# Attention keys as three chunks of 128 and a shared rest of 64, with batch 0 in a written-out order of steps, in an attention and SwiGLU FFN kernel

## The chip, the cores and the metric

The kernel runs on one core of a Trainium2 chip. The metric is the device time of one execution in microseconds (us). Times come from repeated runs; the profile comes from one further execution that the hardware profiler recorded, and it has a time of its own.

## The reference

Softmax attention over 8 batches of 12 heads with 448 tokens and a head dimension of 64, followed by a gated FFN on the 3584 tokens with 768 features. All inputs and the output are float32.

```python
scores = q @ k.T / sqrt(64)                 # per head: 448 x 448
attn = exp(scores - max) / sum              # over keys
x = (attn @ v), heads side by side          # 3584 x 768
out = (silu(x @ w_gate) * (x @ w_val)) @ w_out   # 768 -> 1536 -> 768
```

## The kernel before

The work is cut into 48 pairs of heads, six pairs per batch. Engines: PE is TensorE (PEld its weight loads), DVE is VectorE, ACT is ScalarE, POOL is GpSimd, SP only issues transfers. All matmuls are in fp16 with fp32 sums in PSUM. Every engine runs its instructions in the order in which the program lists them; the order is written by hand and by a small planner at build time.

**One pair.** `load_qk16` and `load_v` load q, k and v with a cast from fp32 to fp16; these transfers are issued by POOL. A partition holds four neighbouring tokens of a head, so 112 partitions hold the 448 tokens, and the keys are taken as four chunks of 112. `prep` brings q and k into the layout `qkT` with the head dimension on partitions: for pairs 0 to 10 with transposes on PE (`turn`, line 199) and one copy on DVE, for pairs 11 and later (`NPE`) with two copies on POOL (line 167) and two transfers with transpose on SP (lines 170 and 174). `qk(pr, c)` makes one score unit: two matmuls with 64 rows each, one per head, in the two halves of TensorE (line 217), and one exp on ACT over both heads (line 225). `pv_chunk` multiplies the exps by v with a column of ones (line 243 and 251): eight matmuls of 65 columns per chunk into one PSUM bank `acc`. The queries of a head are 448 = 3 x 128 + 64; the rests of the two heads share one accumulator slot, with zeros in `E` between the heads. After the last chunk DVE divides by the sums (lines 262 to 274). `turn_x` turns the result into `X`, the input of the FFN: on PE for pairs below `XPE` = 12, on SP from there on. For the first two batches `turn_rests` (line 306) turns the last 64 queries of all six pairs.

**FFN.** The tokens are split into eight blocks of alternately 384 and 512. `ffn1_steps` has twelve steps per block: a group `gp` and a group `vp` of six matmuls each (line 326), a tanh on ACT (line 341) and two operations on DVE (345 and 348). `ffn2_steps` has six or eight steps per block: twelve matmuls into `op` (line 371), an eviction on ACT (378), and after two steps the stores from SP (390).

**PSUM.** [...] Three score buffers of two banks (`ps_s`) and two single banks (`ps_f`, tag `f`) that `acc`, `vp`, `op` and the turns use in rotation; `gp` sits in a score buffer, or in an `f` bank when `gate_small` is set.

**Order.** The first six pairs (`FIRST`) run in a loop over 24 score units, with the turns, V copies (`copy_v`) and PV chunks at places from the tables `XAT` and `CAT`. From then on the program goes through visits: each takes two or three score units, up to two pairs of PV that are ready (`todo`), and then FFN steps. Which FFN steps stand in a visit comes from `run_budget` for the first blocks and from `share` later. Block 0's second half (`ffn2_steps`) follows its first half at once; the second halves of later blocks wait in `ffn2_wait` until the next block is added. A block is added two visits after the PV of its batch's last pair.

**Loads.** The table `wq` says at which pair weights and early pairs are asked for: gate and value weights (`g`, `v`, four parts each) at pairs 0 to 4, the output weights `wo` (`o`) at pairs 6 and 7. Pairs from 14 on are loaded six pairs ahead (`LA`), when the score units of a pair begin. POOL's queue holds all of these loads in order, together with the copies of line 167. In the built program each load from POOL, from the ninth on, waits for the load eight before it.

Of the kernel before, what the change touches and what calls it, by code (L numbers as in the profile page):

```python
# [26 lines left out]
NX = 6  # L27
NV = 5
VS = 9
EB = 15  # L30
# [3 lines left out]
def kernel(  # L34
# [24 lines left out]
    MQ = S - D  # L59
# [13 lines left out]
    load_table("exp_and_others")  # L73

# [7 lines left out]
    ps_f = ctx.enter_context(tc.tile_pool(name="ps_f", bufs=2, space=PSUM))  # L82

    Es = [consts.tile([P, NC * EB + 1, D], FP16, name=f"E{i}") for i in range(NE)]
    Xts = [consts.tile([128, 7, D], FP16, name=f"xt{i}") for i in range(NX)]
    Xrs = [consts.tile([D, 128], FP16, name=f"xr{i}") for i in range(3)]
    Vts = [consts.tile([P, 2, NC, D + 2], FP16, name=f"vo{i}") for i in range(NV)]
    vraw = consts.tile([P, VS, 2, NC, D], FP16, name="vraw")
# [17 lines left out]
    def dummy(n):  # L106
        wp = ps_f.tile([128, 512], FP32, tag="f", name="wp")
        for _ in range(n):
            nc.tensor.matmul(wp[:], lhsT=warm[:, 0:128], rhs=warm[:], start=True, stop=True)  # L109

    def load_qk32(pr):
        rq = raws.tile([P, 2, NC, D], FP32, tag="rq", bufs=RB)
        rk = raws.tile([P, 2, NC, D], FP32, tag="rk", bufs=RB)
        for dst, src in ((rq, q), (rk, k)):
            nc.sync.dma_start(dst[:], src[0, 2 * pr : 2 * pr + 2].rearrange("h (p c) d -> p h (c d)", c=NC))
        raw[pr] = (rq[:], rk[:])
# [3 lines left out]
    def load_qk16(pr, n=2):  # L120
        h0 = 2 * (pr % 2) if pr >= 14 else 0
        if h0 == 0:
            q16 = raws.tile([P, 4, NC, D], FP16, tag="rq", bufs=RB, name="q16")
            k16 = raws.tile([P, 4, NC, D], FP16, tag="rk", bufs=RB, name="k16")
            pairbuf[:] = [q16, k16]
        q16, k16 = pairbuf
        for dst, src in ((q16, q), (k16, k)):
            flat = src.rearrange("b h s d -> (b h) s d")[2 * pr : 2 * pr + 2 * n]
            nc.gpsimd.dma_start(dst[:, ds(h0, 2 * n)], flat.rearrange("h (p c) d -> p h (c d)", c=NC))  # L129
        for i in range(n):  # L130
            h = h0 + 2 * i
            raw[pr + i] = (q16[:, h : h + 2], k16[:, h : h + 2])

    def load_v(pr, n=1):
        b, h = divmod(2 * pr, H)
        nc.gpsimd.dma_start(  # L136
            vraw[:, ds(pr % VS, n)].rearrange("p r h c d -> p (r h) (c d)"),
            v[b, h : h + 2 * n].rearrange("h (p c) d -> p h (c d)", c=NC),
        )
# [17 lines left out]
    def prep(pr):  # L157
        rq, rk = raw[pr]
        if pr == 0 or pr >= NPE:
            qk16 = attp.tile([P, 2, NC, 2, D], FP16, tag="qk16", bufs=3)  # L160
            for t, src in enumerate((rq, rk)):
                dst = qk16[:, 1 - t].rearrange("p c h d -> p h c d")
                if pr == 0:
                    nc.vector.tensor_copy(dst[:, 0], src[:, 0])
                    nc.scalar.activation(dst[:, 1], src[:, 1], AF.Copy)
                else:
                    nc.gpsimd.tensor_copy(dst, src)  # L167
        qkT[pr] = attp.tile([128, 2 * S + D], FP16, tag="qkT", name="qkT", bufs=5)
        if pr >= NPE:
            nc.sync.dma_start_transpose(  # L170
                qkT[pr][:, 0 : 2 * S].rearrange("p (c q) -> p c q", q=P),
                qk16[:].rearrange("p t c h d -> p (t c h d)"),
            )
            nc.sync.dma_start_transpose(
                qkT[pr][:, 2 * S :].rearrange("p (c q) -> p c q", c=1),
                qk16[0:D, 1, 0].rearrange("p h d -> p (h d)"),
            )
            return None

        def turn0():  # L180
            for t in range(2):
                tp = ps_s.tile([128, 2, 512], FP32, tag="s", name="tp")
                for c in range(NC):
                    for hx in range(2):
                        nc.tensor.matmul(
                            tp[ts(hx, 64), c // 2, ds(c % 2 * P, P)],
                            lhsT=qk16[:, 1 - t, c, hx],
                            rhs=ident[0:P, 0:P],
                            start=True,
                            stop=True,  # L190
                        )
                dst = qkT[pr][:, ts(1 - t, S)].rearrange("p (a x) -> p a x", a=2)
                nc.vector.tensor_copy(dst[:, 0], tp[:, 0, 0 : 2 * P])
                nc.scalar.activation(dst[:, 1], tp[:, 1, 0 : 2 * P], AF.Copy)
                if t == 0:
                    tq = tp
            nc.vector.tensor_copy(qkT[pr][:, 2 * S :], tq[:, 0, 0:D])

        def turn():
            if pr < FIRST + 2:  # L200
                tp = ps_s.tile([128, 2, 1024], FP16, tag="s", name="tp")[:, 0]
            else:
                tp = ps_f.tile([128, 1024], FP16, tag="f", name="tp")
            for i in range(2 * NC + 1):
                t, c = (1 - i // NC, i % NC) if i < 2 * NC else (0, 0)
                for hx in range(2):
                    src = raw[pr][t][:, hx, c, :]
                    nc.tensor.transpose(tp[ts(hx, 64), ts(i, P)], src, ident[0:P, 0:P])  # L208
            nc.vector.tensor_copy(qkT[pr][:], tp[:, 0 : 2 * S + D])  # L209
# [3 lines left out]
    def qk(pr, c):  # L213
        t = qkT[pr]
        s = ps_s.tile([128, 2, 512], FP32, tag="s")
        for hx in range(2):
            nc.tensor.matmul(  # L217
                s[:, hx, 0:S],
                lhsT=t[ts(hx, 64), c * P : c * P + 128],
                rhs=t[ts(hx, 64), ds(S + (1 - hx) * D, S)],  # L220
                start=True,
                stop=True,
            )
        e = Es[pr % NE][:, ds(c * EB, 16)].rearrange("p (h b) x -> p h (b x)", h=2)
        nc.scalar.activation(e[:, :, 0:S], s[0:P, :, 0:S], AF.Exp, scale=sm_scale)  # L225

    def qk_half(pr, half, between=None):
        for c in (2 * half, 2 * half + 1):
            qk(pr, c)
            if between and c % 2 == 0:  # L230
                between()
# [3 lines left out]
    def pv_chunk(pr, c):  # L235
        if c == 0:
            accs[pr] = ps_f.tile([128, 512], FP32, tag="f", name="acc")
        e = Es[pr % NE]
        vo = Vts[pr % NV]
        a7 = accs[pr][:, 0 : 7 * (D + 1)].rearrange("p (s d) -> p s d", s=7)  # L240
        for j in range(3):
            for hx in range(2):
                nc.tensor.matmul(  # L243
                    a7[:, 2 * j + hx],
                    lhsT=e[:, ds(c * EB + 9 * hx + 2 * j, 2)].rearrange("p b x -> p (b x)"),
                    rhs=vo[:, hx, c, 0 : D + 1],
                    start=c + j + hx == 0,
                    stop=False,
                )
        for hx in range(2):  # L250
            nc.tensor.matmul(  # L251
                a7[:, 6],
                lhsT=e[:, ds(c * EB + 6 + hx, 2)].rearrange("p b x -> p (b x)"),
                rhs=vo[:, hx, c, 0 : D + 1],
                start=False,
                stop=c == NC - 1 and hx == 1,
            )
        if c < NC - 1:
            return
        r = attp.tile([128, 8], FP32, tag="R", bufs=2, name="R")  # L260
        xt = Xts[pr % NX]
        nc.vector.reciprocal(r[:, 0:7], a7[:, :, D])  # L262
        n = 7 if pr < XPE else 6
        nc.vector.tensor_tensor(  # L264
            xt[:, 0:n],
            a7[:, 0:n, 0:D],
            r[:, 0:n].unsqueeze(2).to_broadcast([128, n, D]),
            ALU.mult,
        )
        if pr < XPE:  # L270
            return
        for hx in range(2):
            nc.vector.tensor_scalar(
                Xrs[pr % 3][:, ts(hx, D)], a7[ts(hx, D), 6, 0:D], r[ts(hx, D), 6:7], None, ALU.mult
            )

    def pv(pr):
        for c in range(NC):
            pv_chunk(pr, c)

    def turn_x(pr):
# [5 lines left out]
        xt = Xts[pr % NX]  # L287
        if pr < XPE:
            tp = accs[pr] if pr < FIRST else ps_f.tile([128, 512], FP32, tag="f", name="xtp")
            for j in range(3):  # L290
                nc.tensor.matmul(  # L291
                    tp[:, ts(j, 128)],
                    lhsT=xt[:, 2 * j : 2 * j + 2].rearrange("p h d -> p (h d)"),
                    rhs=ident[:],
# [3 lines left out]
            nc.vector.tensor_copy(dst[:, 0:MQ], tp[:, 0:MQ])  # L298
            return
        nc.sync.dma_start_transpose(  # L300
            dst[:, 0:MQ].rearrange("p (j q) -> p j q", j=3),
            xt[:, 0:6].rearrange("p j d -> p (j d)"),
        )
        nc.sync.dma_start_transpose(dst[:, MQ:S].rearrange("p (j q) -> p j q", j=1), Xrs[pr % 3][:])

    def turn_rests(b):
        tp = ps_f.tile([128, NHP, D], FP32, tag="f", name="rtp")
# [334 lines left out]
```

The softmax here doesn't subtract the row's maximum and nothing guards it: scores larger than these inputs give would overflow.

## Time and profile before

| what | value |
|---|---|
| median of 3 runs | 453.32 us (453.19 to 453.83) |
| profiled execution | 453.5 us, span 451.7 us, granted PE clock 0.998 |
| PE busy | 441.9 us (98%) |
| ACT busy | 238.8 us (53%) |
| DVE busy | 201.6 us (45%) |
| POOL busy | 141.8 us (31%) |
| transfers | 48.71 MB in packets, mean 108 GB/s |

The span is the time from the first to the last instruction in the profile; about 1.8 us of the profiled time lie outside it. "Busy" counts the time in which an engine works. Matmul ends are modelled, so lengths of matmuls overlap; the distance from one start to the next is the firmer number. In lists of instructions, the bracket at a line's end is the idle time before it and what ended that. For transfers the time from issue to landing is given.

How busy the transfers are in the first part of the span shows in this row of the page, the moved GB/s in 40 slices of 11.3 us (first eight): 142, 173, 200, 201, 196, 172, 174, 180.

### The profile page before, as it was taken

What the parts mean: (1) busy time and instruction counts of PE and PEld (TensorE: products, weight loads), DVE (VectorE), ACT (ScalarE), POOL (GpSimd) and SP (SyncE); (2) the same over time, 40 slices, a digit from 0 to 9 for tenths busy, and PEclk for the clock granted to TensorE, in tenths of its full rate; (3) what the DMA queues carried; (4) which work ended last, traced back from release to release, by engine and by line L of the source; (5) the groups of instructions that cost most, each with busy time, mean ns of one, the idle gap of its engine ahead of it and who ended that gap; (6) DMA issues with size and microseconds to landing.
All of it is one profiled execution on the core that took longest, in us unless ns stands there. A gap on an engine that the chain in (4) does not pass through costs nothing.

```text
span 451.7 us, 9871 instructions
## 1 busy us (share of the span) xinstructions
PE 441.9 (98%) x4024; PEld 247.0 (55%) x4024; DVE 201.6 (45%) x447; ACT 238.8 (53%) x350; POOL 141.8 (31%) x228
## 2 busy tenths in 40 slices
PE   8999999999999999999999999999999999999995
PEld 3655565545455556454555656545455666544563
DVE  3666562456654434455443534353453544055300
ACT  6965666566746465554554546644555462222221
POOL 8755715927642225252313405330100000000000
PEclk9999999999999999999999999999999999999999
DMA  9999999999969379874749758772503112200033
GB/s 142 173 200 201 196 172 174 180 209 119 145 93 133 46 129 124 132 120 71 126 74 120 98 78 143 118 105 68 101 20 68 46 46 57 70 2 0 17 100 95
DMA packets 105101, 48.71 MB, mean 108 GB/s; under 512 B 59744, under 2 KB 101600, under 8 KB 105056
## 3 DMA queue, kind: packets, MB, share of 16 engines
q0 software_dynamic: 43392, 23.37, 41.2%
q1 hardware_dynamic: 61664, 24.71, 28.9%
q8 instruction: 31, 0.51, 0.5%
q14 instruction: 14, 0.11, 0.1%
HBM read 47.19 MB, written 11.01 MB: 129 GB/s over the span
## 4 chain that ended last, share of the span: by engine, by line
PE 93%; DVE 3%; ACT 2%; issue 1%; DVEq 0%; ACTq 0%
PE op L371 24%; PE gp L326 23%; PE vp L326 23%; PE s L217 9%; PE acc L243 9%; PE acc L251 2%; ACT E L225 2%; PE tp L208 1%; PE wp L109 1%; DVE t L345 1%; ACT sg L341 1%; DVE qkT L209 0%; DVE xt L264 0%; PE acc L291 0%; DVE hts L348 0%
## 5 line engine op out<-in xcount | busy, mean ns | idle before, releaser
L225 ACT ACTIVATE E<-s 112x896 f16<-112x896 f32 x192 | 162.1, 919 | 27.5 <-PE s L217 27.4
L326 PE MATMUL gp<-X,wg 128*128 128x384 f16 (+1 forms) x576 | 124.7, 352 | 0.0
L326 PE MATMUL vp<-X,wv 128*128 128x384 f16 (+1 forms) x576 | 124.6, 352 | 0.0
L371 PE MATMUL op<-wo,hts 128*128 128x384 f16 (+1 forms) x684 | 116.1, 323 | 0.0
L345 DVE SCALAR_TENSOR_TENSOR t<-sg,gp 128x384 f32<-128x384 f32 (+1 forms) x96 | 59.7, 621 | 121.8 <-ACT sg L341 121.8
L341 ACT ACTIVATE sg<-gp 128x384 f32<-128x384 f32 (+1 forms) x96 | 52.5, 547 | 84.8 <-PE gp L326 83.6
L371 PEld LDWEIGHTS <-hts 128*128 128x128 f16 x684 | 65.5, 98 | 45.9 <-issue 3.9
L326 PEld LDWEIGHTS <-wv 128*128 128x128 f16 x576 | 56.3, 98 | 52.6
L326 PEld LDWEIGHTS <-wg 128*128 128x128 f16 x576 | 53.1, 97 | 45.6 <-issue 1.1
L378 ACT ACTIVATE osb<-op 128x384 f32<-128x384 f32 (+1 forms) x57 | 27.8, 487 | 92.5 <-PE op L371 92.5
L167 POOL COPY qk<-q 112x512 f16<-112x512 f16 x37 | 22.9, 619 | 144.5 <-DMA qkT<-qk 143.1
L348 DVE SCALAR_TENSOR_TENSOR hts<-t,vp 128x384 f16<-128x384 f32 (+1 forms) x96 | 59.6, 621 | 10.0
L243 PEld LDWEIGHTS <-E 112*128 112x128 f16 x1152 | 46.7, 97 | 18.2 <-issue 17.5
L243 PE MATMUL acc<-vo,E 112*128 112x65 f16 x1152 | 53.0, 193 | 1.3 <-DVE vo L142 0.7
L217 PE MATMUL s<-qkT 64*128 64x448 f16 x384 | 50.6, 355 | 0.2
L251 PE MATMUL acc<-vo,E 112*128 112x65 f16 x384 | 42.9, 193 | 0.0
L262 DVE RECIPROCAL R<-acc 128x7 f32<-128x7 f32 x48 | 9.8, 205 | 70.6 <-PE acc L251 70.5
L129 POOL DMA_DIRECT2D k<-in_k_dram x44 | 29.0, 660 | 9.5 <-DMA wo<-in_moe_w_out_dram 7.8
L129 POOL DMA_DIRECT2D q<-in_q_dram x44 | 29.3, 666 | 5.2 <-PE s L217 2.5
L136 POOL DMA_DIRECT2D vraw<-in_v_dram x42 | 28.0, 666 | 8.4 <-DVE vo L142 7.2
L217 PEld LDWEIGHTS <-qkT 64*128 64x128 f16 x384 | 14.5, 94 | 25.8 <-issue 18.6
L264 DVE TENSOR_TENSOR xt<-acc,R 128x384 f16<-128x384 f32 (+1 forms) x48 | 27.6, 574 | 1.7
(41 smaller groups left out, 148.2 us busy)
## 6 DMA issues: line engine op xcount, KB each, us to landing
q<-in_q_dram POOLq DMA_DIRECT2D x41, 112.0 KB, 4.0
k<-in_k_dram POOLq DMA_DIRECT2D x41, 112.0 KB, 4.6
vraw<-in_v_dram POOLq DMA_DIRECT2D x39, 112.0 KB, 4.6
wg<-in_moe_w_gate_dram POOLq DMA_DIRECT2D x8, 288.0 KB, 10.1
wv<-in_moe_w_val_dram POOLq DMA_DIRECT2D x8, 288.0 KB, 10.2
wo<-in_moe_w_out_dram POOLq DMA_DIRECT2D x2, 1152.0 KB, 22.0
out_dram<-osb SPq DMA_DIRECT2D x8, 288.0 KB, 3.0
out_dram<-osb SPq DMA_DIRECT2D x8, 240.0 KB, 3.1
```

The source lines that it names most:

```text
L129: nc.gpsimd.dma_start(dst[:, ds(h0, 2 * n)], flat.rearrange("h (p c) d -> p h (c d)", c=NC))
L136: nc.gpsimd.dma_start(vraw[:, ds(pr % VS, n)].rearrange("p r h c d -> p (r h) (c d)"), v[b, h : h + 2 * n].rearrange("h (p c) d -> p h (c ...
L217: nc.tensor.matmul(s[:, hx, 0:S], lhsT=t[ts(hx, 64), c * P : c * P + 128], rhs=t[ts(hx, 64), ds(S + (1 - hx) * D, S)], start=True, stop=True,)
L225: nc.scalar.activation(e[:, :, 0:S], s[0:P, :, 0:S], AF.Exp, scale=sm_scale)
L243: nc.tensor.matmul(a7[:, 2 * j + hx], lhsT=e[:, ds(c * EB + 9 * hx + 2 * j, 2)].rearrange("p b x -> p (b x)"), rhs=vo[:, hx, c, 0 : D + 1] ...
L251: nc.tensor.matmul(a7[:, 6], lhsT=e[:, ds(c * EB + 6 + hx, 2)].rearrange("p b x -> p (b x)"), rhs=vo[:, hx, c, 0 : D + 1], start=False, st ...
L326: nc.tensor.matmul(dst[:, 0:n], lhsT=wslice(kind, fb, cb), rhs=X[kk][:, cb, ds(c0, n)], start=(cb == 0), stop=(cb == NCB - 1),)
L341: nc.scalar.activation(sg[:, 0:n], gp[:, 0:n], AF.Tanh, scale=0.5)
L345: nc.vector.scalar_tensor_tensor(t1[:, 0:n], sg[:, 0:n], 1.0, gp[:, 0:n], ALU.add, ALU.mult)
L348: nc.vector.scalar_tensor_tensor(hts[:, fb, 0:n], t1[:, 0:n], 0.5 * HS, vp[:, 0:n], ALU.mult, ALU.mult)
L371: nc.tensor.matmul(op[:, 0:w], lhsT=hts[:, fb, ts(ch, 128)], rhs=wo[oh][:, fb, ds(m0 - oh * OH, w)], start=(fb == 0), stop=(fb == NFB - 1),)
L378: nc.scalar.activation(osb[:, ds(m0, w)], op[:, 0:w], AF.Copy, scale=1.0 / HS)
```

## The change

**Keys.** The 448 keys of a head become three chunks of 128 and a rest of 64. K and V are loaded onto 128 partitions with two transfers of 64 partitions each (`load_keys`), whose rows overlap, so that each of the four token columns holds 128 keys. For one head of a pair the rest is the low half of the first column, for the other it is the high half of the last column (`low`). The rest of both heads of two neighbouring pairs makes one score unit `(pr, RU)`: four matmuls of 64 x 64 in the four quarters of TensorE, and one exp into a shared buffer `Ers`. Two pairs then have seven score units instead of eight. PV has for each head and chunk four matmuls, three chunks with 128 rows and the rest with 64 rows; the four query slots need no zeros any more, and `turn_rests` goes. Each head has its own accumulator bank, so a pair takes two.

**Early pairs.** K of pairs below 11 is loaded as seven tokens per partition (`halves`), with the heads of a pair on the two halves of the partitions, and is turned with 16 transposes of 64 x 64.

**Order.** Batch 0 follows the string `START`: s a score unit, t a turn of q and k, v a V copy, p a PV piece, x a turn of X. It has its own two-bank PSUM buffer `ps_a`, which is given back as the two `f` banks when the visits begin. X turns of batch 0 use score buffers. It ends with the first two score units of pair 6. A visit takes at most one pair of PV, and the rest piece of it comes right behind the score units. Block 0's second half waits for block 1 like all others. From block 1 on, `add_block` sets beforehand how many FFN1 and FFN2 steps each visit has; a visit ahead of a PV gets an FFN2 step at its end. The turns of X and of pairs up to 10 come right after the next FFN1 step. The loads of `wo` move from pairs 6 and 7 to pairs 8 and 9; pairs 10 and 11 are loaded singly.

**Other edits.** q of pair 0 is loaded from ACT's queue and k from SP's, the table load comes behind them. `NX` goes from 6 to 3. The stores are cut by 112 rows from the start of a batch.

```diff
-            0: [("qk", 6), ("g", 0), ("v", 0)],
...
-            6: [("V", 3), ("o", 0)],
-            7: [("o", 1)],
+            6: [("V", 3)],
+            8: [("o", 0)],
+            9: [("o", 1)],
```

```diff
+    def load_keys(eng, dst, src, h0, n):
+        for s in range(2):
+            rows = bass.AP(
+                src.tensor, (h0 * S + s * KR) * D, [[(2 * NC - 1) * D, 64], [S * D, n], [1, NC * D]]
+            )
+            eng.dma_start(dst[ts(s, 64)], rows)
...
     def qk(pr, c):
         s = ps_s.tile([128, 2, 512], FP32, tag="s")
+        if c < KR:
+            t = qkT[pr]
+            for hx in range(2):
+                nc.tensor.matmul(
+                    s[:, hx, 0:S],
+                    lhsT=t[ts(hx, 64), ts(c + low(pr, hx), 128)],
+                    rhs=t[ts(hx, 64), ds(NC * 128, S)],
...
+            e = Es[pr % NE][:, c]
+        else:
+            for hx in range(2):
+                for p in (pr, pr + 1):
+                    lo = low(p, hx)
+                    t = qkT[p]
+                    nc.tensor.matmul(
+                        s[ts(1 - lo, 64), hx, 0:S],
+                        lhsT=t[ts(hx, 64), ds(0 if lo else KR * 128 + 64, 64)],
+                        rhs=t[ts(hx, 64), ds(NC * 128, S)],
...
+            e = Ers[pr // 2 % NR][:]
...
+    def pv_mm(pr, hx, c, j):
+        lo = low(pr, hx)
...
+        if c < KR:
+            rows, e, col = slice(0, 128), Es[pr % NE][:, c], c + lo
+        else:
+            rows, e, col = (slice(0, 64), Ers[pr // 2 % NR], 0) if lo else (slice(64, 128), Ers[pr // 2 % NR], KR)
+        nc.tensor.matmul(
+            accs[pr][0][hx][:, ts(j, D + 1)],
+            lhsT=e[rows, ds(hx * S + j * 128, 128)],
+            rhs=Vts[pr % NV][rows, hx, col, 0 : D + 1],
...
+            else:
+                accs[pr] = ([fbank(), fbank()], [0, 0])
...
+START = (
+    "sstssvtsppsppstvsxsvpspppstsppsppsvtsspp"
+    "pvxspsxspppvpstsppxsppsxx"
+)
...
+                for pr, c in sorted(chunks, key=lambda x: -(x[1] == RU)):
+                    qk(pr, c)
+                for _, p0 in todo:
+                    pv_piece(p0, RU)
...
-            (oq if i == 0 else ffn2_wait).extend(own)
+            ffn2_wait.extend(own)
```

## The prediction

> **What bounds the kernel now.** I read the page first, then the chain that ended last, then the order in time of PE, ACT, POOL and the transfers in the first 100 us, where the change does most.
>
> ```profile
> span 451.7 us, 9871 instructions
> PE 441.9 (98%) x4024; PEld 247.0 (55%) x4024; DVE 201.6 (45%) x447; ACT 238.8 (53%) x350; POOL 141.8 (31%) x228
> ...
> PE 93%; DVE 3%; ACT 2%; issue 1%; DVEq 0%; ACTq 0%
> ...
> L225 ACT ACTIVATE E<-s 112x896 f16<-112x896 f32 x192 | 162.1, 919 | 27.5 <-PE s L217 27.4
> ```
>
> PE carries 93% of the chain, so outside the start a gain is what leaves PE's queue, and a loss is what makes PE wait. ACT is half idle, so 24 fewer exps are worth nothing there. The start is different:
>
> ```profile
> 6.59 5.04 ACT L225 ACTIVATE E<-s 112x896 f16<-112x896 f32 x6 [0.42 <-PE s L217]
> 11.83 8.39 ACT L225 ACTIVATE E<-s 112x896 f16<-112x896 f32 x10 [0.19 <-PE s L217]
> ```
>
> From 6.6 us ACT runs exps back to back, 8.39/10 = 0.84 us apiece; the first FFN group starts at 29.79. Next, one steady visit in order of time (start, length, instruction):
>
> ```profile
> 198.33 2.11 PE L371 MATMUL op<-wo,hts 128*128 128x384 f16 x12
> ...
> 200.38 0.74 PE L217 MATMUL s<-qkT 64*128 64x448 f16 x6
> 200.48 0.49 ACT L378 ACTIVATE osb<-op 128x384 f32<-128x384 f32 x1 [2.65 <-PE op L371]
> ...
> 201.05 0.35 PE L243 MATMUL acc<-vo,E 112*128 112x65 f16 x6
> ...
> 202.02 1.46 PE L326 MATMUL gp<-X,wg 128*128 128x512 f16 x6
> ```
>
> Ends are modelled, so I use starts. Six gp matmuls of 512 columns take 1.29 us to the next start: 0.42 ns a column. The three score units (six matmuls of 448) take 0.67 us: 3 x 0.187 = 0.56, one pass per two heads, and 0.11 to leave the mode; 0.10 was spent to enter it. The 32 PV matmuls take 0.97 us, 30 ns each. Last, POOL's queue and the transfers (for issue lines of transfers: number, median us to landing, here in 51 to 54, 60 to 66 and 110 to 130 us):
>
> ```profile
> 51.77 0.61 POOL L167 COPY qk<-q 112x512 f16<-112x512 f16 x1 [1.37 <-DMA q<-in_q_dram]
> 52.94 0.62 POOL L167 COPY qk<-k 112x512 f16<-112x512 f16 x1 [0.56 <-DMA k<-in_k_dram]
> ...
> 64.97 0.66 POOL L129 DMA_DIRECT2D k<-in_k_dram  x1 [7.75 <-DMA wo<-in_moe_w_out_dram]
> ...
> 73.42 0.62 POOL L167 COPY qk<-q 112x512 f16<-112x512 f16 x1
> ```
> ```profile
> qkT<-qk SPq DMA_TRANSPOSE x2, 10.5
> ...
> qkT<-qk SPq DMA_TRANSPOSE x2, 12.9
> ...
> qkT<-qk SPq DMA_TRANSPOSE x7, 3.0
> ```
>
> Pair 12 lands at 52 us, although it was issued at 40.5. From 20 to 60 us the transfers move 190 to 200 GB/s without a gap, and a transpose started in 51 to 66 us needs 10 to 13 us, against 3 later. Each load from POOL waits for the load eight issues earlier, so one late wo stops POOL for 7.75 us. Pair 14 is copied at 73.4, its transposes land near 80.5, and PE first uses them at 84.75. No PE time is lost, but the margin is 4 us of a phase that is full.
>
> [...] two 64-row heads take one pass, and the switch costs 0.1 us each way. For column tiles the 112x64 transposes start 25 to 27 ns apart where 112 columns at 0.42 ns would be 47. Four 64x64 tiles at once no run here shows. [...] in the rows a 112x64 load takes 109 ns, a 128x128 load 98, so a small loss. [...]
>
> **The change part by part.**
>
> *Scores.* Three units of 128 keys per pair, and one rest unit per two pairs: 3.5 instead of 4. Per batch of six pairs 21 x 0.187 = 3.93 us instead of 24 x 0.187 = 4.49, if the rest's four quadrant matmuls share one pass. Visits of three units: 7 instead of 8, saving 0.21. The three rest units add a switch from quadrants to halves: 0 to 0.1 each, taken 0.05.
> *PV.* Still 32 matmuls a pair, but the 8 of the rest have 64 rows on alternating halves. Bounds for the 8: 65 columns x 0.42 x 4 = 0.11 us, or 0.24 if nothing overlaps; I take 0.14, because the 64-column matmuls at L310 start about 17.5 ns apart (12 in 0.31 us, 0.1 of it switch). Per batch 6 x (24 x 0.0303 + 0.14) = 5.2 instead of 5.82.
> *Two accumulators* now take both small PSUM banks, so the second waits for the eviction of the last op or vp. After an op: eviction ends at 200.97, the scores at 200.94, so 0 to 0.1 per visit, 0.3 per batch. After a vp, as in all of batch 0's FFN: about 0.3 a visit.
> Sum per batch: 3.93 + 7 x 0.21 + 0.15 + 5.2 + 0.3 = 11.05. Before it was 12.07 (two batches from 235.89 to 341.75 are 105.86 us, less 81.73 of FFN). So -1.0 a batch; for the 34 pairs after the early phase **-5.8** (0 if neither the rest's scores nor its PV overlap, -8 at best).
>
> *Start.* 21 exps instead of 24 before batch 0's X: -2.5. Given back: V of pair 0 comes in two issues, its copy now stands ahead of pair 2's turn on DVE, and PV(0) queues ahead of score unit 5 on PE; turns and X turns take score buffers. I take 0.7 back: **-1.8** (-3 to +1.5), FFN at 28.0. Weights g0, v0 are issued 1.6 us later (two more POOL issues of 0.66) and land near 26.5 (10.7 after 15.8), so that is covered by 1.5 us, and what goes over is PE wait. POOL's cover for the other extra issues (5 instead of 3 per pair, +1.3 us) is its waiting (143 us on transposes); it is absent only early. The casts and the table load stay under the first load's landing (1.6 us idle): nothing either way within 0.5.
>
> *Early phase, 28 us to the start of batch 1's FFN.* Before, FFN2 of block 0 (six groups, 11.7 us) stood here; now it follows with block 1. PE's own work in visits 0 to 10: 12 FFN1 steps x 1.95 = 23.4; 27 units 5.0; switches 2.0; 7 PV 6.7; six X turns 1.8; four turns 2.2; bank waits 2: 43, so batch 1 could begin at 71. In the same measure before is at 84.95 (84.75 and the one unit more that is done) - 11.7 = 73.2. So PE asks for pair 14 at 67.5 instead of 84.75, and for pair 12 at 58.5 instead of 71.7. The transfers can't follow:
> - Pair 12: bytes ahead of it are as before or a little more (keys and values overlap, 128 partitions for 112), so it lands at 52 again. Two copies 1.3, two transposes issued 2.5, landing 6 to 10: 62 to 66. Wait of 3.5 to 7.
> - Pair 14: its copies stand on POOL behind K of pair 16, that waits eight issues back for o0. o0 now goes out near 50, behind 0.43 MB more, and lands at 65 (62.5 to 67). Three more issues, copies to 68.3, transposes issued to 70.8, landing 6.5 (4 to 10): PE has it at 77 (73 to 81).
> - The rest of that visit 3.5: batch 1 begins at 80.5. Its first unit is the rest of 14 and 15, and pair 15 stands behind o1 (near 74): 1.5 (0 to 5) more: 82 (75 to 87).
> What waits behind: PE in order, so PV, FFN1 and all else; the V copies on DVE (V13 behind o1, landing near 76) come in that same time and add nothing.
> Balance: 82 + 11.7 - 84.95 = **+8.8** (+2 to +14), the -1.8 of the start contained and lost in it.
>
> *Rests and tail.* The two rest turns (0.4 us each with their waits) lie in the early phase. The last rows leave on two queues instead of two transfers on SP: -0.3 (-0.6 to +0.2). SP has as many transposes as before, four a pair, with more equal sizes: nothing, covered by transposes landing tens of us ahead after 110 us.
>
> Sum: +8.8 - 5.8 - 0.3 = +2.7. The profiled execution is 453.5 (span 451.7 and 1.8 around it), the median 453.32; so **456.0**.
>
> **Rivals.**
> 1. *Forecast: early transfers become the bound.* 456; with the bounds of its parts 454.3 to 462. For it: the full 190 to 200 GB/s, the 7.75 us wait for wo, the 4 us margin. Against: the o loads are asked for two pairs later, and fewer bytes stand before pair 14.
> 2. *Transfers keep up (other side).* Without them 71 + 11.7 - 84.95 = -2.3, then -6.1: 445; with half the wait about 450. It decides where o0 lands: break-even is batch 1 beginning at 79.3, that is pair 14's scores by about 74.5 with no wait for pair 15. Transposes landing in 4 to 5 us, as at 73 to 77 us before, would do it.
> 3. *Quadrants and halves don't overlap.* Then -5.8 becomes 0, with late transfers 462; with timely ones about 451.
> 4. *Bank waits after vp* of 1 us instead of 0.3 in seven visits: 5 us, but only where transfers are in time, so 450 instead of 445.
>
> **How the numbers follow.** About 0.2% (0.9 us) is what a measurement of this kernel can tell from no change. Forecast 0.55 and rival 3 with late transfers 0.07 are slower; rival 2 0.26 and its variants with 3 or 4 0.07 are faster; 0.05 between. So faster 0.33, same 0.05, slower 0.62. Range 446 to 462; the likeliest case's own is 454 to 462.
>
> **What would show it.** Right: PE idle of some us before score units near 58 to 82 us, released by qkT transposes; POOL waiting for wo; the PV of a pair at 0.87 us plus a switch; start of FFN near 28. Wrong: PE without gaps there and batch 1's first 512-column group near 72; or a rest unit of 0.37 us instead of 0.19.

## The result and the profile after

The changed kernel takes **470.0 us** (median of 4 runs, 467.63 to 472.19) against 453.28 us: a ratio of **1.0365** (95% interval 1.0313 to 1.0418). It is slower, as forecast, but by 16.7 us and not by 2.7, and outside the range. The profiled execution is the slowest of the four, 472.19 us, its span 470.4, so 18.7 us more than before's span; the sums below are made against these spans.

First the page of the changed kernel: the span, the engines' busy times, PE and its granted clock in 40 slices of 11.8 us, and the chain that ended last.

```profile
span 470.4 us, 10050 instructions
PE 440.8 (94%) x4076; PEld 247.9 (53%) x4076; DVE 200.4 (43%) x459; ACT 218.3 (46%) x326; POOL 183.2 (39%) x306
...
PE   8999288699999999999999999999999999999997
...
PEclk9999779799999999999999999999999999999999
...
PE 79%; DMA 9%; ACT 5%; POOL 2%; DVE 2%; issue 2%; DVEq 0%; ACTq 0%; POOLq 0%
```

PE's busy time is the same (440.8 against 441.9; some of it now runs at a granted clock of 0.50 to 0.61, see below), so the loss is waiting. Most of it lies between 47 and 94 us: PE is 20% busy in the fifth slice and 60% in the eighth, and the clock is down in the fifth, sixth and eighth slices. Transfers, on no step of the chain before, now have 9% of it. Here is PE in order of time in that stretch (start, length, instruction, idle time before it and what ended that):

```profile
26.72 1.20 PE L388 MATMUL f<-X,wg 128*128 128x384 f16 x6
...
49.90 1.14 PE L388 MATMUL gp<-X,wg 128*128 128x384 f16 x6
...
59.72 2.08 PE L388 MATMUL f<-X,wv 128*128 128x384 f16 x6 [8.68 <-DVE R L335]
...
80.76 0.37 PE L262 MATMUL s<-qkT 64*128 64x448 f16 x2 [1.19 <-DMA qkT<-qk]
...
88.85 0.58 PE L275 MATMUL s<-qkT 64*64 64x448 f16 x3 [4.52 <-DMA qkT<-qk]
...
91.76 2.75 PE L388 MATMUL gp<-X,wg 128*128 128x512 f16 x6
...
95.78 1.46 PE L388 MATMUL gp<-X,wg 128*128 128x512 f16 x6
```

The FFN begins at 26.72 us (29.79 before), so the start gains 3.1. The first `gp` group of 512 columns, where block 1 begins, starts at 91.76. In before it starts at 86.40, with the second half of block 0 (11.7 us) already done, from 67.56 on:

```profile
67.56 4.07 PE L371 MATMUL op<-wo,hts 128*128 128x384 f16 x24
...
86.40 1.46 PE L326 MATMUL gp<-X,wg 128*128 128x512 f16 x6
```

So 86.40 - 11.7 = 74.7 is the comparable time: the early phase as a whole loses **17.1 us**. From there to the end it is 378.6 us, against 451.7 - 86.40 + 11.7 = 377.0 before: **+1.6**. The two make the 18.7.

The gap of 8.68 us is put down to DVE's reciprocal, because that belongs to the division that frees the accumulator's bank. DVE itself had waited, as its order in time says, for V of pair 9:

```profile
58.63 0.40 DVE L171 COPY vo<-vraw 128x512 f16<-128x512 f16 x1 [9.94 <-DMA vraw<-in_v_dram]
58.95 0.16 DVE L335 RECIPROCAL R<-f 128x4 f32<-128x4 f32 x1
```

and POOL's order shows when that load went out, and what it did next:

```profile
46.08 1.43 POOL L125 DMA_DIRECT2D vraw<-in_v_dram  x2 [1.95 <-DVE xt L336]
...
53.59 1.04 POOL L184 DMA_DIRECT2D wo<-in_moe_w_out_dram  x1 [1.74 <-issue]
...
67.47 0.60 POOL L125 DMA_DIRECT2D k<-in_k_dram  x1 [4.43 <-DMA wo<-in_moe_w_out_dram]
...
77.96 0.59 POOL L125 DMA_DIRECT2D k<-in_k_dram  x1 [4.93 <-DMA wo<-in_moe_w_out_dram]
...
79.88 0.63 POOL L200 COPY qk<-k 128x512 f16<-128x512 f16 x1
```

V of pairs 9 to 11 is issued at 46.08 in two loads of 192 KB, which took 11.3 us to land while 200 GB/s were moved. The copies for pair 15 stand behind K loads that wait for `wo`, and come at 79.88; its transposes end the gap of 4.52 us at 88.85. After both long gaps PE works at half speed for a while, which the windows show (length of the stretch, busy time and count of PE, PEld, DVE, ACT, POOL, then clock, DMA share and GB/s):

```profile
55.00:60.00 5.00, 0.28 (x2) 0.15 (x3) 1.30 (x5) 0.00 (x0) 3.90 (x7) 0.50 1.37 192
60.00:65.00 5.00, 5.00 (x52) 3.04 (x51) 2.35 (x7) 2.31 (x3) 3.05 (x5) 0.61 1.28 192
...
90.00:95.00 5.00, 5.00 (x43) 2.81 (x40) 1.21 (x4) 2.47 (x4) 5.00 (x9) 0.53 1.59 169
```

In 60 to 65 and 90 to 95 us PE is busy throughout, but at the granted clock (1 - 0.61) x 5 + (1 - 0.53) x 5 = 4.3 us of its work do not get done there, an estimate from these two clocks. The six matmuls at 59.72 are listed with 2.08 us where those at 49.90 have 1.14.

### The profile page after: what moved, and what is told of

Its sections match the earlier page's. It is cut to its first block, busy times and chain, and to the rows that moved or that the text cites. A ratio compares the mean times of both kernels' runs of the same rounds, so it can differ in the third digit from the quotient of the medians.

```text
span 470.4 us, 10050 instructions
## 1 busy us (share of the span) xinstructions
PE 440.8 (94%) x4076; PEld 247.9 (53%) x4076; DVE 200.4 (43%) x459; ACT 218.3 (46%) x326; POOL 183.2 (39%) x306
## 4 chain that ended last, share of the span: by engine, by line
PE 79%; DMA 9%; ACT 5%; POOL 2%; DVE 2%; issue 2%; DVEq 0%; ACTq 0%; POOLq 0%
PE f L433 23%; PE f L388 21%; PE gp L388 20%; PE f L297 8%; PE s L262 5%; DMA wo<-in_moe_w_out_dram 4%; DMA vraw<-in_v_dram 4%; ACT E L283 3%; DMA qkT<-qk 1%; PE s L275 1%; DVE t L407 1%; POOL vraw L125 1%; ACT er L283 1%; ACT sg L403 1%; PE acc L297 1%
## 5 line engine op out<-in xcount | busy, mean ns | idle before, releaser
L388 PE MATMUL f<-X,wv 128*128 128x384 f16 (+1 forms) x576 | 125.8, 355 | 8.7 <-DVE R L335 8.7
L283 ACT ACTIVATE E<-s 128x896 f16<-128x896 f32 x144 | 123.1, 925 | 16.9 <-PE s L262 16.6
L433 PE MATMUL f<-wo,hts 128*128 128x384 f16 (+1 forms) x684 | 115.8, 323 | 5.5 <-DVE t L407 5.5
L388 PE MATMUL gp<-X,wg 128*128 128x512 f16 (+1 forms) x516 | 113.6, 357 | 0.0
L407 DVE SCALAR_TENSOR_TENSOR t<-sg,gp 128x512 f32<-128x512 f32 (+1 forms) x86 | 53.7, 624 | 91.6 <-ACT sg L403 91.6
L403 ACT ACTIVATE sg<-gp 128x512 f32<-128x512 f32 (+1 forms) x86 | 47.5, 552 | 87.1 <-PE gp L388 85.7
L410 DVE SCALAR_TENSOR_TENSOR hts<-t,f 128x384 f16<-128x384 f32 (+1 forms) x96 | 59.6, 621 | 11.5 <-PE f L388 1.3
L297 PEld LDWEIGHTS <-E 128*128 128x128 f16 x1152 | 38.5, 98 | 4.0 <-issue 1.2
L297 PE MATMUL f<-vo,E 128*128 128x65 f16 x1008 | 38.7, 195 | 0.0
L336 DVE TENSOR_TENSOR xt<-f,R 128x256 f16<-128x256 f32 x84 | 35.7, 424 | 2.9
```

The source lines that it names most:

```text
L283: nc.scalar.activation(e[:, 0 : 2 * S].rearrange("p (h q) -> p h q", h=2), s[:, :, 0:S], AF.Exp, scale=sm_scale)
L297: nc.tensor.matmul(accs[pr][0][hx][:, ts(j, D + 1)], lhsT=e[rows, ds(hx * S + j * 128, 128)], rhs=Vts[pr % NV][rows, hx, col, 0 : D + 1], ...
L336: nc.vector.tensor_tensor(xt[:, :, hx], a4[:, :, 0:D], r[:].unsqueeze(2).to_broadcast([128, KR + 1, D]), ALU.mult,)
L388: nc.tensor.matmul(dst[:, 0:n], lhsT=wslice(kind, fb, cb), rhs=X[kk][:, cb, ds(c0, n)], start=(cb == 0), stop=(cb == NCB - 1),)
L403: nc.scalar.activation(sg[:, 0:n], gp[:, 0:n], AF.Tanh, scale=0.5)
L407: nc.vector.scalar_tensor_tensor(t1[:, 0:n], sg[:, 0:n], 1.0, gp[:, 0:n], ALU.add, ALU.mult)
```

## The experiments

They ask two things: which wait sets the pace of the early phase (V of pair 9, the number of loads on POOL, the weights ahead of pair 14, or the missing cover of block 0's second half), and where the forecast saving of the steady visits went. "After" stands for the changed kernel, "before" for the other. Before's median was 453.2 to 453.3 us each time.

**V of pairs 9 to 11 asked for earlier** (after, ahead of weight part 2).

```diff
-            3: [("qk", 9, 1), ("qk", 10, 1), ("qk", 11, 1), ("g", 2), ("v", 2)],
+            3: [("qk", 9, 1), ("qk", 10, 1), ("qk", 11, 1), ("V", 3), ("g", 2), ("v", 2)],
...
-            6: [("V", 3)],
```

> The changed kernel with one load moved: V of pairs 9 to 11 is asked for ahead of the weight parts 2 and 3 instead of behind them. Theory A (the 8.7 us gap of PE from 50.9 to 59.7 us is DVE's 9.9 us wait for V of pair 9, and the half clock after it costs 2 us more): that gap goes; since PE then asks for the keys of pairs 12 to 15 about 10 us sooner, a part comes back as waits for qkT: 462 us (457 to 467), DVE's wait for vraw under 2 us. Theory B (the bytes that must have moved by batch 1 set the pace, whatever their order): 468 to 471, the gap moves to qkT. Theory C (two accumulator banks and the modes on PE cost the time): 469 to 471, no change in the order of waits elsewhere.

Measured: 471.56 us, 1.0389 (1.0337 to 1.044), no gain. PE in order of time:

```profile
58.53 0.38 PE L275 MATMUL s<-qkT 64*64 64x448 f16 x3 [1.96 <-DMA qkT<-qk]
...
69.70 0.93 PE L262 MATMUL s<-qkT 64*128 64x448 f16 x4 [6.27 <-DMA qkT<-qk]
...
77.22 0.38 PE L275 MATMUL s<-qkT 64*64 64x448 f16 x3 [2.00 <-DMA qkT<-qk]
...
89.88 0.38 PE L275 MATMUL s<-qkT 64*64 64x448 f16 x3 [4.12 <-DMA qkT<-qk]
```

This is theory B. The gap of 8.68 us is gone, and the same time is lost in gaps before score units: 1.96 + 6.27 + 2.00 + 4.12 = 14.35 us in all, where after has 8.68 + 1.19 + 4.52 = 14.39. The largest gap of a trace is therefore not the cause by itself: behind it stood a chain of transfers with its own pace.

**The same, and `wo` four pairs later** (pairs 12 and 13 instead of 8 and 9), so that two transfers of 1152 KB leave the way of pairs 14 and 15.

```diff
-            8: [("o", 0)],
-            9: [("o", 1)],
+            12: [("o", 0)],
+            13: [("o", 1)],
```

> The changed kernel with V of pairs 9 to 11 ahead of weight parts 2 and 3 (alone 471.6, no gain) and the wo loads moved from pairs 8 and 9 to pairs 12 and 13. Theory B' (the bytes in the queue ahead of a needed load set the pace; wo is 2.36 of them, 12 us at 190 GB/s): the gaps of 6.3 and 4.1 us on qkT of pairs 12 and 15 shrink to under 2 each and part of the half clock goes: 460 us (456 to 465). If the chain of copies, issue and transposes on POOL and SP is the limit: 468 to 472.

Measured: 462.58 us, 1.0197 (1.018 to 1.0213), 9.0 less than with V earlier alone. The time came as expected, the gaps only in part:

```profile
67.26 0.93 PE L262 MATMUL s<-qkT 64*128 64x448 f16 x4 [4.88 <-DMA qkT<-qk]
...
83.39 1.46 PE L388 MATMUL gp<-X,wg 128*128 128x512 f16 x6
```

The waits for pairs 13 and 15 are gone, so these came from `wo` on the way. (The one for pair 11 is gone too, but this profile also begins its FFN 2.8 us later than the one above, at 29.19 us.) The wait for pair 12 shrank only from 6.27 to 4.88 us, where under 2 was expected: K of pair 12 is issued behind the gate and value parts 2 and 3, and POOL waited 7.2 us for it before it could copy.

**Fewer loads on POOL** (after; q and k from pair 14 and V from pair 12 for two pairs at once, so 2.5 issues a pair instead of 5).

```diff
-                if 14 <= pr + LA < NPAIR:
-                    load_qk16(pr + LA, 1)
+                if 14 <= pr + LA < NPAIR and (pr + LA) % 2 == 0:
+                    load_qk16(pr + LA, 2)
```

> The changed kernel with q, k (from pair 14) and v (from pair 12) of two pairs in one set of loads: the same bytes, 2.5 POOL loads a pair instead of 5, so that the wait for the load eight back reaches further and the copies of pairs 14 and 15 no longer stand behind a wait for wo. Theory F' (the halved loads make POOL wait for wo ahead of the copies; this gave the 4.5 us gap at 84 and the half clock after it): POOL's waits for wo (9.4 us) and the gap at 84 go, the 8.7 us gap for V of pair 9 stays: 464 us (461 to 467). If bytes alone set the pace: 468 to 472.

Measured: 464.05 us, 1.0227 (1.0207 to 1.0246).

```profile
59.73 2.08 PE L388 MATMUL f<-X,wv 128*128 128x384 f16 x6 [8.78 <-DVE R L335]
...
84.62 1.46 PE L388 MATMUL gp<-X,wg 128*128 128x512 f16 x6
```

The bytes are the same, yet the gap before the rest of 14 and 15 is gone: that unit starts at 82.75 instead of 88.85. The gap for pair 9 stays. The expected reason is not what the trace shows. POOL still waits for `wo`, 13.5 us in all against 9.4 in after:

```profile
61.93 0.65 POOL L200 COPY qk<-k 128x512 f16<-128x512 f16 x1
...
69.11 0.61 POOL L125 DMA_DIRECT2D vraw<-in_v_dram  x1 [5.43 <-DMA wo<-in_moe_w_out_dram]
69.72 0.63 POOL L200 COPY qk<-k 128x512 f16<-128x512 f16 x1
...
80.22 0.61 POOL L125 DMA_DIRECT2D k<-in_k_dram  x1 [8.08 <-DMA wo<-in_moe_w_out_dram]
```

But with fewer issues between them, the copies of pair 14 (61.93) stand ahead of the wait for the first `wo` part and those of pair 15 (69.72) ahead of the wait for the second. In after each stands behind it, at 70.67 and 79.88.

**The extra loads alone, in before** (V loads, and K loads from pair 11, cut in two of 56 partitions each).

```diff
+            cuts = (0, 56, P) if src is k and pr >= NPE else (0, P)
...
+        for lo, hi in ((0, 56), (56, P)):
+            nc.gpsimd.dma_start(
+                vraw[lo:hi, ds(pr % VS, n)].rearrange("p r h c d -> p (r h) (c d)"), rows[lo:hi]
+            )
```

> The kernel before with every V load and the K loads from pair 11 on cut into two of 56 partitions each: five POOL loads a pair instead of three, nothing else. Theory A' (it is the earlier demand): 453 to 455, the margin of the early phase covers them. Theory F (the extra issues and the shorter reach of the wait eight loads back make the loads late): 458 or more, with PE gaps between 45 and 90 us.

Measured: 460.99 us, 1.0166 (1.0151 to 1.0181), although no byte and no score changed. POOL in order of time:

```profile
65.87 0.63 POOL L141 DMA_DIRECT2D vraw<-in_v_dram  x1 [6.59 <-DMA wo<-in_moe_w_out_dram]
...
73.05 0.62 POOL L141 DMA_DIRECT2D vraw<-in_v_dram  x1 [6.55 <-DMA wo<-in_moe_w_out_dram]
73.66 0.62 POOL L171 COPY qk<-q 112x512 f16<-112x512 f16 x1
```

This is theory F. Both halves of one V load now have a `wo` part eight issues back. The copies of pair 13, at 55.45 us in before, stand behind them at 73.66, and PE waits 5.28 us for its transposes, until 80.54.

**Block 0's second half behind its first again** (after), and **the reverse in before**.

```diff
-            ffn2_wait.extend(own)
+            (oq if i == 0 else ffn2_wait).extend(own)
```

> The changed kernel with block 0's second FFN half back in block 0's visits, as in the kernel before; loads of wo stay at pairs 8 and 9. Theory A' (attention of pairs 9 to 15 is asked for too soon because 11.7 us of FFN2 no longer stand ahead of it): PE reaches pair 9's PV near 53 instead of 49 us, so a gap of about 4 to 5 us is left there, and none or under 2 us at 84; the second half waits for wo part 1 a little: 460 us (455 to 465). Theory C (banks, modes): 467 to 471.

> The kernel before with one edit: block 0's second FFN half waits for block 1, as in the changed kernel; all loads stay where they are (wo at pairs 6 and 7). Theory A' (earlier demand alone makes the loads late): PE waits for V or qkT of pairs 12 to 15 between 50 and 85 us, and the clock falls after it: 460 us (456 to 466). Theory C or the split loads as the cause: 453 to 454.5, no gaps.

Measured: after with the old order 461.51 us, 1.0181 (1.0163 to 1.0199), so 8.5 less; before with the new order 461.94 us, 1.0191 (1.0168 to 1.0214), so 8.7 more. Both came as expected, and the two agree on the size. The waits of before with the new order from 28 to 100 us (total, times, longest):

```profile
DVE vo L142 <- DMA vraw<-in_v_dram: 7.2, 2, 4.5
```

In before it is V alone that comes late; no score unit waits as much as 0.5 us for a transpose. In after the second half also brings the transposes in time: with it back, PE's waits for pairs 14 and 15 (1.19 and 4.52 us) are gone, and the one for V of pair 9 shrinks from 8.68 to 5.22.

So the 11.7 us of matmuls had been cover for late loads, in two ways. For pairs 11 and later the matmuls stand ahead of their score units or PV (in before from 67.56 on). For the earlier pairs, V of pair 9 among them, they don't. There the order works through `run_budget`, which gives each visit its share of all FFN work still left: with the second half in block 0's visits, nine FFN1 steps stand ahead of the PV of pair 8 in before, without it six. In after it is six, and eight with the old order.

**Both costs in before at once**: cut loads and the waiting second half, with before's scores, PV and start.

> The kernel before with both: every V load and the K loads from pair 11 cut in two halves of 56 partitions (so 5 issues per pair on POOL), and block 0's second half waiting for block 1. Alone these gave +7.7 and +8.7 us. Theory G (two costs that add up: the second half's 11.7 us was the cover that hid late transfers, and the halves make POOL and so the transfers later still): 468 to 471, which would be the whole difference of the changed kernel made without its scores, PV or START. Rival (they are one wait seen twice, the later transfer decides and covers the other): 461 to 464. In between, part of the one lies in the wait of the other.

Measured: 469.77 us, 1.0378 (1.036 to 1.0396). The single costs of 7.7 and 8.7 us add up, to the changed kernel's time. PE in order of time:

```profile
57.76 0.34 PE L295 MATMUL xtp<-ident,xt 128*128 128x128 f16 x3 [3.83 <-DVE xt L268]
...
60.25 2.11 PE L330 MATMUL gp<-X,wg 128*128 128x384 f16 x6
...
79.66 0.56 PE L221 MATMUL s<-qkT 64*128 64x448 f16 x2 [6.48 <-DMA qkT<-qk]
...
91.17 1.46 PE L330 MATMUL gp<-X,wg 128*128 128x512 f16 x6
```

Two long gaps, a stretch at a granted clock of 0.50 after each (in 60 to 62 and in 80 to 82 us), and the first 512-column group at 91.17: nearly the changed kernel's picture (91.76). It shows that these two edits are enough for the loss of the early phase. It does not show that the changed kernel's parts are the same two: that one starts its FFN 3.1 us sooner and loses 1.6 us in the steady part, where this one takes 467.8 - 91.17 = 376.6 us against 377.0 in before.

**Both undone in after.**

> The changed kernel with only these two undone: block 0's second half follows its first half again, and q, k from pair 14 and v from pair 12 are loaded for two pairs at once. Alone they gave -8.5 and -6.0 us. Theory G (they add up): 455 to 457.5. Rival (one wait, undone twice): 460 to 462, as with the first alone; then the wait for V of pair 9 and the stall in visits without PV carry the rest.

Measured: 461.69 us, 1.0183 (1.0169 to 1.0197). This went to the rival: in after the two gains do not add. With the second half back, having fewer issues gains nothing more. 8.4 us are left against before. One part is the stall in visits without PV, which comes next; another is the wait for V of pair 9, which stands where it was:

```profile
59.73 2.10 PE L388 MATMUL f<-X,wv 128*128 128x384 f16 x6 [4.77 <-DVE xt L336]
```

**Visits without PV.** In such a visit the exps are in the way: `gp` sits in an `f` bank, its tanh stands behind three exps on ACT, and the next `op` waits for that bank. After, PE in order of time, one such visit:

```profile
169.04 0.38 PE L275 MATMUL s<-qkT 64*64 64x448 f16 x4
169.36 0.55 PE L262 MATMUL s<-qkT 64*128 64x448 f16 x4
169.84 1.15 PE L388 MATMUL f<-X,wg 128*128 128x384 f16 x6
170.83 1.14 PE L388 MATMUL f<-X,wv 128*128 128x384 f16 x6
173.09 2.11 PE L433 MATMUL f<-wo,hts 128*128 128x384 f16 x12 [1.12 <-DVE t L407]
```

The edit puts the FFN2 step ahead of the FFN1 step there:

```diff
+                if bare and no:
+                    run_o()
+                    no -= 1
                 for _ in range(nf):
                     run_fv()
```

> The changed kernel with another order in the visits without PV from block 1 on: the FFN2 step stands ahead of the FFN1 step instead of behind it. Theory D (in such a visit gp sits in a small bank, the FFN2 step behind it needs that bank while the tanh is queued behind three exps, so PE waits 0.7 to 1.1 us once per batch): the waits of L433 on DVE t go, 0.2 to 0.3 come back at the next PV's second bank: about 4 to 5 us less, 465 us (462.5 to 467.5). Rival (the wait only moves to the next PV, which needs both banks): 469 to 471.

Measured: 465.15 us, 1.0261 (1.0228 to 1.0294), 4.9 less, as expected. The same visit with the edit has no gap:

```profile
165.10 0.55 PE L262 MATMUL s<-qkT 64*128 64x448 f16 x4
165.58 2.12 PE L433 MATMUL f<-wo,hts 128*128 128x384 f16 x12
167.54 1.14 PE L388 MATMUL f<-X,wg 128*128 128x384 f16 x6
```

From the first 512-column group to the end this kernel takes 462.1 - 89.25 = 372.9 us. The three runs that keep the old order there and have no half-speed stretch behind that point (late `wo`, fewer loads, and the next one; their groups of 512 columns start 1.29 to 1.30 us apart) take 377.3 to 377.4. So the stall is worth about 4.4 us; after's waits list 5.5, and about 1.2 comes back as short waits of PV for its bank. (The profile is also 2.5 us ahead at that group, 89.25 against 91.76. Up to there the two kernels list the same order of work, so this is scatter of the early phase.)

**The half clock by itself.** Matmuls of zeros fill both long gaps, so that the clock stays up; they write nothing that is used.

```diff
+                if x == 11:
+                    dummy(17)
...
+            if x == 5:
+                dummy(34)
```

> The changed kernel with matmuls on a block of zeros in the two long gaps of PE: 34 of 512 columns behind the PV of pair 8 (7.3 us into the 8.7 us gap) and 17 ahead of the score units of the first visit of block 1 (3.7 us into the gap at 84). Nothing of the real work is moved. Theory E (after a gap PE is granted about half the clock for some 4 us): the clock stays up, the work from 59.7 to 64.5 and from 88.9 to 95.8 us takes 2 and 2.5 us less: 466 us (464.5 to 467.5). Without such an effect: 470 to 471.

Measured: 470.25 us, 1.037 (1.0355 to 1.0386), no gain in the medians, so theory E is out. The clock did stay up, at 1.00 behind both gaps; in 55 to 60 us:

```profile
55.00:60.00 5.00, 3.44 (x18) 1.52 (x17) 0.92 (x5) 0.49 (x1) 3.88 (x7) 1.00 1.36 191
```

But PE then came earlier to the next transfer, and waited there: pair 14's scores start at 80.41 against 80.76, the rest unit at 89.09 against 88.85. Only the half-speed stretch behind the last gap can count, and its 2.4 us in the two profiles (468.0 against 470.4) are within the scatter of after's runs. So here the clock lost ahead of a late transfer cost nothing of its own; whether the last stretch costs 2 us stays open in the medians.

**Putting the fixes together.** Two kernels: the second half back, the FFN2 step first in visits without PV, and V of pairs 9 to 11 earlier; and the same with the loads for two pairs at once.

> The changed kernel with three edits together: block 0's second FFN half back in block 0's visits (alone 461.5), the FFN2 step ahead of the FFN1 step in visits without PV (alone 465.2 against 470), and V of pairs 9 to 11 asked for ahead of weight parts 2 and 3. If the causes add up: 461.5 - 4.9 = 456.6, and the 5.2 us gap at 54 to 60 us that stayed in the run with the FFN half back, with about 1.5 us of half clock, goes too, since the demand is now late enough for the bytes: 450 us (447 to 454), below the kernel before. If the bytes still set the pace, the gap only moves: 455 to 458.

> The changed kernel with four edits: block 0's second FFN half back in its visits, FFN2 ahead of FFN1 in visits without PV, loads of two pairs together, and V of pairs 9 to 11 behind weight part 2 and ahead of part 3 (ahead of part 2 a vp group waited 1.7 us for its weights). Against the run with three edits (454.2) the weight wait (1.7) and 1 us on qkT at 70 go: 451.5 us (449.5 to 454), below the kernel before by 0.4%. If another wait takes their place: 453.5 to 455.

Measured: 454.21 us, 1.002 (1.0004 to 1.0036), and 454.56 us, 1.002 (1.0006 to 1.0035). Neither beats before: the first lies just above its expected range, the second went to its rival. That these edits take back nearly all of the 16.7 us, with the new scores, PV and start in place, is what rules out theory C, that banks and modes are the main cost. In both profiles the first 512-column group starts 2.4 us later than before's 86.40 (88.76 and 88.78), behind short waits for weights and for PV's bank; from there to the end they take 362.7 us against 365.3. What the changed kernel saves in the steady part is 2.7 us in these two profiles, and the early phase takes it.

## Why the prediction was wrong in size

- **Start.** -1.8 forecast, -3.1 measured in the profile of after, FFN at 26.72 instead of 28.0. As forecast it is lost in the waits that follow.
- **Early transfers, the mechanism.** Right: POOL waits for `wo` and PE for transposes, and the forecast loss was in this phase. The first `wo` part went out at 53.59 (forecast near 50), the loads behind the two parts went on at 67.47 (65) and 77.96 (74), and pair 14's scores came at 80.76 (77): each 2.5 to 4 us later.
- **Early transfers, the size: the step that failed.** Batch 1 began at 88.85 and not at 82, past the range of 75 to 87. In the prediction's own measure the early phase cost 88.85 + 11.7 - 84.95 = +15.6 instead of +8.8. The term that fails is pair 15. For pair 14 the prediction added 12 us from the landing of `wo` to the scores (65 to 77). Pair 15 stands behind the second part in the same way, but was given "1.5 (0 to 5) more" behind pair 14's visit. By the working for pair 14 it would have come at 74 + 12 = 86, so 4 of the 6.8 us were missing in the sum itself. Measured are 77.96 to 88.85, which is 10.9 us, and a wait of 4.52; the other 3 us come from `wo`, whose second part landed 4 us later than forecast. The run with fewer loads shows that this is the place: with the copies of pair 15 ahead of the wait for the second part, the unit starts at 82.75.
- **Five issues per pair.** Their price was 1.3 us a pair behind an idle queue, "absent only early", and for pair 14 three more issues. Their cost was another: they set which load is eight back, and so which copies stand behind a wait for `wo`. Halving them gained 6.0 us in after, adding them cost 7.7 in before.
- **Early transfers, the first link.** Wrong: pair 12 was taken for the first late load. It was V of pair 9, issued at pair 6 as before, behind weight parts 2 and 3, and needed earlier since fewer FFN1 steps stand ahead of it. The prediction looked at the V copies from pair 13 on and called them covered. The wait of 3.5 to 7 us that it forecast for pair 12 did not come, for this gap had held PE back before. The earlier V load shows that this link alone is not what the sum was short of: without this wait the time is lost at the next links.
- **The second half of block 0.** The prediction saw that without it PE asks for pair 14 at 67.5 instead of 84.75. Between its two cases, transfers in time (-2.3) and late (+8.8), lie 11.1 us. Undoing the move gained 8.5 us and doing it in before cost 8.7, so its price was seen, but not that V of pair 9 would pay part of it.
- **The clock.** The sum priced waits at their length, and work after a long one ran at half speed: the six matmuls behind the gap of 8.68 us are listed with 2.08 us where those ahead of it have 1.14, and the granted clock is 0.50 in 55 to 60 us and 0.61 in 60 to 65. Which gaps lower it is not settled by these runs (last section). Ahead of 88.85 the lost clock cost nothing of its own, as the zeros showed. Behind it, the stretch to the first 512-column group takes 91.76 - 88.85 = 2.91 us where the run with zeros takes 1.66 (89.09 to 90.75). That makes most of the 1.5 us between +15.6 and the +17.1 above.
- **Steady visits.** -5.8 and -0.3 for the rest forecast, +1.6 measured, so 7.7 are missing. The term left out is the FFN2 step of the visits without PV: 5.5 us of waits in six places, of which the run with FFN2 first shows about 4.4 to be lost time. About 1.4 more is the half clock behind 91.76 (0.53 in 90 to 95 us): two groups take 95.78 - 91.76 = 4.02 us, against 2.59 in before. The rest, some 2 us, is small: the rest unit takes 0.32 us to the next start where 0.187 + 0.05 was taken (17 x 0.08 = 1.4), a pair of PV 0.90 (1.01 from the start at 213.52 us to the next group, less the 0.11 of the change of mode), where 0.87 was taken (34 x 0.03 = 1.0). These two are read from the trace only.

The row of after's waits that carries the steady term (engine, line, what ended it: total, times, longest):

```profile
PE f L433 <- DVE t L407: 5.5, 6, 1.1
```

- **Rivals.** Rival 2 (transfers keep up) is out. Rival 3 is out as far as the scores go: the four quadrants take 0.32 us with their change of mode, less than the 0.37 of two passes. Rival 4 stayed small: PV waited for its two banks 0.42 + 0.47 us in the visit at 71 us and 0.35 in the one at 75, 1.2 us in the whole early phase where the rival had up to 1 us in each of seven visits.

What stays open: how much of the 16.7 us belongs to the issues and how much to the second half, since in after the two overlap (6.0 and 8.5 us alone, 8.3 together). And after and its variants, which share one start, begin the FFN near 26.7 us in most profiles and near 29 in two (28.91 and 29.19), with the first score units spread differently; nothing in these runs says what sets it.

## What to carry to other kernels

Before work is moved out of a full phase, ask what lands behind it: moving 11.7 us of it cost 8.5 to 8.7 us here. Ask it for every load, not only for those that look latest: the first one to be late was not on the list. A queue whose issues wait for an issue so many back has a reach in issues, so cutting a load in two can cost there even where no byte is added and the queue looks idle (7.7 us in before). What counts is which instructions stand behind the wait. And follow each late wait to the load that ended it, then to the next late load in the same queue: fixing only the first one gave nothing.

## What the hardware showed that was not expected

- Nine of the traces have windows of 2 to 6 us at and behind twelve PE gaps of 3.51 to 8.68 us. At each gap the lowest of them has a mean granted clock of 0.50 to 0.73 (0.50 at seven). Read as a mix of 1.00 and 0.50, the means come to some 3 to 6 us of work at 0.50 behind each gap, an estimate. For gaps of about 2 us the length did not decide: behind 1.99 us (at 70.08 in before with both costs) and 2.00 us (at 77.22 with V earlier) the windows show 1.00; behind 1.96 us (at 58.53 with V earlier) 60 to 62 us has 0.50, and behind 2.06 us (at 86.34 with FFN2 first) 85 to 90 us has 0.66. What decided there, these runs do not show. Two windows of the run with V earlier, behind its gaps of 1.96 and 2.00 us:

```profile
60.00:62.00 2.00, 2.00 (x8) 0.91 (x6) 0.07 (x1) 1.90 (x3) 2.00 (x4) 0.50 1.31 204
...
75.00:80.00 5.00, 3.00 (x47) 1.91 (x46) 2.38 (x7) 2.36 (x3) 0.59 (x1) 1.00 1.25 150
```

- Matmuls of 64 x 64 in all four quarters overlapped: four of 448 columns took 0.32 us to the next start (66.69 to 67.01 us in after), less than two passes of 0.187. If they share one pass, about 0.13 us is left for the change of mode, an estimate from these two numbers.
- A load of V of 192 KB took 11.3 us to land (after, issued at 46.08 us) while 200 GB/s were moved.
